# Sparse attention and a PReLU feed-forward on one core: score pieces joined per head pair, crossbar transposes for all four pairs, another order in batches 0 and 1

## The chip, the core and the metric

The kernel runs on one core of one Trainium2 chip. The core has a matrix engine (TensorE, PE in the profile), a vector engine (VectorE, DVE), a scalar engine (ScalarE, ACT), GpSimd (POOL), and a queue processor, SyncE (SP), which here only issues DMAs. The metric is the device time of one execution in microseconds; less is better. Before the change the median of seven runs is 329.11 us (328.95 to 331.41).

## What is computed

Eight batches of eight heads, 576 positions of 64 elements each. The first four heads attend to the last 32 positions (local), the last four to all earlier positions with the same remainder modulo 32 (strided). Softmax, product with v, and then a feed-forward over all 4608 positions with a per-channel leaky slope:

```python
scores = scale * np.matmul(q, k.transpose(0, 1, 3, 2))
mask_local = (rel >= 0) & (rel < stride)                # stride = 32
mask_strided = (rel >= 0) & (pos[None, :] % stride == pos[:, None] % stride)
masks = np.stack([mask_local if h < H // 2 else mask_strided for h in range(H)], axis=0)
scores = np.where(masks[None, :, :, :], scores, -1000000000.0)
attn = exp(scores - max); attn = attn / (sum(attn) + 1e-09)
attn_out = np.matmul(attn, v)
x = attn_out.transpose(0, 2, 1, 3).reshape(B * S, H * D)     # 4608 x 512
h = x @ w_in                                                 # 512 -> 2048
g = np.maximum(h, 0.0) + alpha * np.minimum(h, 0.0)
out = g @ w_out                                              # 2048 -> 512
```

Inputs and output are float32; the kernel works in float16 with float32 sums.

## The kernel before

**Feed-forward.** The 4608 positions are cut into nine chunks of 512. For each chunk `lin1_piece` (L534) makes one of 16 row blocks of h with four 512-column matmuls (the four operands are the four head pairs' rows of xT), ScalarE makes the negative part (L554), and VectorE combines both (L557). `lin2_piece` (L563) makes the output in 16 parts of four matmuls each, a ScalarE copy to osb after every fourth part (L590), and a transfer out on SP's queue (L591). A chunk therefore has 32 slots: 16 of lin1, 16 of lin2. xT is a ring of four batches.

**Attention.** A head pair is two heads side by side on the 128 partitions. Per batch, pairs 0 and 1 are local and pairs 2 and 3 strided; pair number g is 4 x batch + pair. The work on a pair is cut into pieces:

- T (`transpose_piece`, L221): transposes q or k on TensorE into a "ps" buffer, copies by VectorE and ScalarE, and for k the tails. From batch 2 on (DX = 2) the strided q and k come transposed by the DMA crossbar (`load_d` L118 and `transpose_d` L124), so only the local ones have T pieces.
- S (`score_piece`, L275): half of a pair's scores. The operands have 64 rows (one head), so the two heads' matmuls go to the two halves of the array, each to a bank of its own: TensorE is in a row-tiled mode for this. An exponential on ScalarE (L319) follows, and from batch 2 on a mask multiplication on GpSimd (L329). In batches 0 and 1 the mask is added by two more matmuls (L311).
- P (`pv_piece`, L331): product with v, two pieces for a local pair and three for a strided one, into a "ps" buffer; reciprocal and scaling by VectorE (L352, L354) into x16.
- X: the result is transposed into xT, either on TensorE with a copy by ScalarE or VectorE (`x_piece`, L359), or by a crossbar transpose from SP's queue (`x_dma`, L372): straight into xT for local pairs, into xs for strided ones, with a ScalarE copy later (`x_copy`, L381). Before the change pairs 0, 1 and 2 of batches 2 to 7 use the crossbar, pair 3 uses TensorE.

PSUM[...]: three "ps" buffers (T, tails, P, X), three "hps" (lin1, lin2), and one "sp" of two banks (scores).

**Order.** The order is written by hand: `alone` (L406) lists the pieces of batches 0 and 1, and the loop at L449 lists those of later batches. In pass g of that loop, pair g is scored, pair g - 1 gets its products with v, and the next local unit is transposed; `run` (L490) adds to a piece the casts, loads and crossbar transposes that go with it. `attn_step` (L524) issues the next piece after a lin1 or lin2 slot, and then the VectorE part of lin1 that was put off (`late`). Batch 0 runs ahead of all chunks with warm-up matmuls between the pieces (L662); batch 1 in the lin2 half of chunk 0; batch n + 1 in chunk n (L708), paced by

```python
acc += left / (22.5 - 0.5 * skip) * (0.5 if i < 16 else 1.0)
```

so that pieces come half as densely in lin1 as in lin2 and the last one falls about one slot before the end of the chunk. Lin1 of chunk n reads xT of batch n, finished at the end of chunk n - 1. Chunks 7 and 8 have no attention beside them. [...]

Of the kernel before, what the change touches and what calls it, by code (L numbers as in the profile page):

```python
# [31 lines left out]
def kernel(  # L32
# [10 lines left out]
    nc = tc.nc  # L43
# [46 lines left out]
    vls = [cpool.tile([128, 24, 65], F16, name=f"vl{i}") for i in range(2)]  # L90
    vss = [cpool.tile([128, 4, 8, 65], F16, name=f"vs{i}") for i in range(2)]
    ets = [cpool.tile([128, 640], F16, name=f"et{i}") for i in range(NE)]
    x16s = cpool.tile([80, 1024], F16)
    qks = {nm: cpool.tile([80, 4, 512], F16, name=f"{nm}sd") for nm in "qk"}


# [105 lines left out]
    def make_pair(g):  # L202
        P = Pair()
        P.g, P.b, P.hp = g, g // 4, g % 4
        P.strided = P.hp >= 2
        P.pr = P.hp % 2
        P.n, P.w = (8, 72) if P.strided else (6, 96)
        u = g // 2
        P.dx = P.b >= DX and P.strided
        P.xd = P.b >= DX and P.hp < 3  # L210
        if P.dx:
            P.qT, P.kT = (z[u % 2].rearrange("r e c -> r (e c)") for z in (qTs, kTs))
        else:
            P.qT, P.kT = qTs[u % 2][:, g % 2], kTs[u % 2][:, g % 2]
        P.sgroups = ([0, 1, 2, 3], [4, 5, 6, 7]) if P.strided else ([0, 1, 2], [3, 4, 5])
        P.pgroups = ([0, 1, 2], [3, 4, 5], [6, 7]) if P.strided else P.sgroups
        P.et = {}
        P.x16 = None
        return P
# [55 lines left out]
    def score_piece(P, i):  # L275
# [52 lines left out]
            m = (mstr if P.strided else mother).unsqueeze(1).to_broadcast([r, 2 * n // w, w])  # L328
        keep(nc.gpsimd.tensor_tensor(ev, ev, m, op=ALU.mult))  # L329

    def pv_piece(P, a):  # L331
        if P.x16 is None:
            if P.xd and P.strided:
                P.x16 = x16s
            else:
                P.x16 = xpool.tile([128, 1024], F16, tag="x16", name="x16")
        v16 = cast16[(P.b, P.strided, "v")]
        grp = P.pgroups[a]
        r = 72 if P.strided else 128
        pv = pspool.tile([128, 512], F32, tag="ps", name="pv")  # L340
        nb = 2 * len(grp)
        for x in range(nb):
            t, hh = grp[x // 2], x % 2
            et, c = P.et[(t, hh)]
            keep(nc.tensor.matmul(  # L345
                pv[:, 65 * x : 65 * x + 65], et[0:r, c : c + 128],
                v16[0:r, 2 * P.pr + hh, t, :] if P.strided else v16[:, 6 * (2 * P.pr + hh) + t, :],
                start=(x == 0), stop=(x == nb - 1), skip_group_check=True))
        w = P.w
        rc = rpool.tile([128, 8], F32, tag="rc", name="rc")  # L350
        pvv = pv[0:w, 0 : 65 * nb].rearrange("r (c e) -> r c e", e=65)
        keep(nc.vector.reciprocal(rc[0:w, 0:nb], pvv[:, :, 64]))  # L352
        c0 = 128 * grp[0]
        keep(nc.vector.tensor_tensor(  # L354
            P.x16[0:w, c0 : c0 + 64 * nb].rearrange("r (c e) -> r c e", e=64),
            pvv[:, :, 0:64],
            rc[0:w, 0:nb].unsqueeze(2).to_broadcast([w, nb, 64]), op=ALU.mult))

    def x_piece(P):  # L359
        xp = pspool.tile([128, 1024], F16, tag="ps", name="xp")  # L360
        for t in range(P.n):
            keep(nc.tensor.transpose(  # L362
                xp[:, P.w * t : P.w * t + P.w], P.x16[0 : P.w, 128 * t : 128 * t + 128], ident[0 : P.w, 0 : P.w]))
        base = (P.b % 4) * S
        if P.strided:
            keep(nc.scalar.copy(  # L366
                xT[:, P.hp, base : base + S].rearrange("r (p t) -> r p t", t=8),
                xp[:, 0:576].rearrange("r (t p) -> r p t", t=8)))
        else:
            keep(nc.vector.tensor_copy(xT[:, P.hp, base : base + S], xp[:, 0:576]))  # L370

    def x_dma(P):  # L372
        base = (P.b % 4) * S
# [29 lines left out]
    def X(g):  # L403
        return lambda: x_piece(pairs[g])

    def alone(u0, u1, ahead):  # L406

        A, L = (2 * u0, 2 * u0 + 1), (2 * u1, 2 * u1 + 1)
        feed(T(u0, "q"), -1)
        feed(T(u0, "k"), -1)  # L410
        for g in A:
            for i in range(2):
                feed(Sc(g, i), -1)
        if ahead:
            feed(T(u1, "q"), -1)
            feed(T(u1, "k"), -1)
            for i in range(2):
                feed(Sc(L[0], i), -1)
        for g in A:
            for i in range(3):  # L420
                feed(Pv(g, i), -1)
        if not ahead:
            feed(T(u1, "q"), -1)
            feed(X(A[0]), -1)
            feed(T(u1, "k"), -1)
            feed(X(A[1]), -1)
            for i in range(2):
                feed(Sc(L[0], i), -1)
        for i in range(2):
            feed(Sc(L[1], i), -1)  # L430
        if ahead:
            for g in A:
                feed(X(g), -1)
        for g in L:
            for i in range(2):
                if g == L[0] and i == 0:
                    feed(lambda: (over_v(u0 // 2, "dve"), pv_piece(pairs[L[0]], 0)), -1)
                else:
                    feed(Pv(g, i), -1)
        for g in L:  # L440
            feed(X(g), -1)

    alone(1, 0, True)
    end0 = len(pieces)
    alone(3, 2, True)
    end1 = len(pieces)


    for g in range(7, npair + 2):  # L449
        c = g // 4  # L450
        a, p, t = g, g - 1, g + 1
        okA = 8 <= a < npair
        okP = 8 <= p < npair
        okT = 8 <= t < npair and (t % 4 == 0 or t < 4 * DX and t % 2 == 0)
        nP = len(pairs[p].pgroups) if okP else 0
        seq = []
        if okA:
            seq.append(("S", Sc(a, 0)))
        if okP:
            seq.append(("P", Pv(p, 0)))  # L460
        if okT:
            seq.append(("T", T(t // 2, "q")))
        if 8 <= g - 2 < npair and not pairs[g - 2].xd:
            seq.append(("X", X(g - 2)))
        if okA:
            seq.append(("S2", Sc(a, 1)))
        if okP:
            seq.append(("P", Pv(p, 1)))
        if okT:
            seq.append(("Tk", T(t // 2, "k")))  # L470
        if nP == 3:
            seq.append(("P", Pv(p, 2)))
        if not seq:
            seq.append(("N", lambda: None))

        todo = [(c, pr) for pr in range(2)] if g % 4 == 0 and 8 <= g < npair else []

        if g % 4 == 1 and 9 <= g and c + 1 < B:
            todo = [(c + 1, nm) for nm in "qk"]
        lastP = max([i for i, z in enumerate(seq) if z[0] == "P"], default=len(seq) - 1)  # L480
        copyP = next((i for i, z in enumerate(seq) if z[0] == "S2"), 0)
        nslots = [i for i, z in enumerate(seq) if z[0][0] != "S"] or list(range(len(seq)))
        for i, (kind, fn) in enumerate(seq):
            extra = []
            if todo and i in nslots:
                left = len([z for z in nslots if z >= i])
                cnt = -(-len(todo) // max(1, left))
                extra = [todo.pop(0) for _ in range(min(cnt, len(todo)))]

            def run(fn=fn, extra=extra, g=g, c=c, kind=kind, lastp=(i == lastP), copyp=(i == copyP)):  # L490
                fn()
                for b, pr in extra:
                    if pr in ("q", "k"):
                        cast_l(b, pr)
                        if b + 1 < B:
                            load_qk(b + 1, False, pr)
                        continue
                    cast_v(b, pr, "pool")
                    if pr == 1 and b + 1 < B:
                        load_v(b + 1, True)  # L500
                if kind == "Tk" and g % 4 == 3 and c + 3 < B:
                    load_tail(c + 3, False)
                if lastp:
                    if 4 * DX <= g - 1 < npair and pairs[g - 1].xd:
                        x_dma(pairs[g - 1])
                    if g % 4 == 0 and DX <= c < B:
                        transpose_d()
                    if g % 4 == 2 and DX <= c and c + 1 < B:
                        load_d(c + 1)
                    if g % 4 == 2 and c + 2 < B:  # L510
                        load_v(c + 2, False)
                if copyp and 4 * DX <= g - 2 < npair and pairs[g - 2].xd and pairs[g - 2].strided:
                    x_copy(pairs[g - 2])
            feed(run, g - 2 if kind == "X" else -1)

    pos = {"i": 0}

# [6 lines left out]
    def attn_step(end):  # L524
# [2 lines left out]
            pos["i"] += 1  # L527
        while late:
            late.pop(0)()


    gTs = {}
# [86 lines left out]
    keep(nc.vector.memset(wrm, 0.0))  # L619
    for nm in "qk":  # L620
        keep(nc.vector.memset(qks[nm][64:80], 0.0))
    keep(nc.vector.memset(x16s[64:80], 0.0))
    keep(nc.sync.dma_start(consts, consts_dram))
    load_qk(0, True, "q")
    load_qk(0, True, "k")
# [129 lines left out]
```

The softmax here doesn't subtract the row's maximum and nothing guards it: scores larger than these inputs give would overflow.

## Time and profile before

| from the profiled execution | |
|---|---|
| its own time | 329.18 us |
| span | 327.2 us |
| TensorE busy | 317.2 us (97%) |
| VectorE / ScalarE / GpSimd busy | 182.6 / 172.6 / 141.4 us |
| lin2 matmuls (L585) | 560, 137.7 us |
| lin1 matmuls (L544) | 640, 133.5 us |
| score matmuls (L295), 72 and 96 columns wide, in sp | 392, 16.9 us |
| exponentials (L319) | 56, mean 646 ns |
| mask multiplications (L329) | 48, mean 1276 ns |
| ScalarE copy xs to xT (L383) | 6, mean 1301 ns |
| ScalarE copy PSUM to xT (L366) | 10, mean 644 ns |
| crossbar transposes xs<-x16s, issue to landing | 6, median 2.7 us |

A line of the timeline gives start, duration (both us), engine, source line, operation, result and operands, shapes, and the number of instructions merged; in brackets, how long the engine was idle before and what ended that. In the chain of work that ended last, each step is followed back to what released it. Matmuls overlap, so their durations add up to more than the time they take: the distance between starts is the measure.

### The profile page before, as it was taken

The numbers are of one execution on the slowest core, as the hardware profiler recorded it, in microseconds if no ns is written. First come the engines' busy times: TensorE is split into PE (matmuls) and PEld (weight loads), VectorE is DVE, ScalarE is ACT, GpSimd is POOL, SyncE is SP. The second block draws the span as 40 slices with busy tenths as digits, with TensorE's granted clock in tenths as the row PEclk, the third lists the DMA queues.
The fourth block names the chain that finished last, engine by engine and source line by source line (L and its number), as shares of the span: only waits on it lengthen the run. The fifth ranks groups of instructions, "written<-read, shape, count | busy, mean of one in ns | idle before, by whom it ended". The sixth has DMA issues, their size and how long they took to land.

```text
span 327.2 us, 6269 instructions
## 1 busy us (share of the span) xinstructions
PE 317.2 (97%) x2493; PEld 161.8 (49%) x2493; DVE 182.6 (56%) x358; ACT 172.6 (53%) x295; POOL 141.4 (43%) x152
## 2 busy tenths in 40 slices
PE   7899999999997999999999999999999999999995
PEld 2454455554553445444558754445444454444444
DVE  5477835577543882388328833783377338505801
ACT  2744663368346754575467645764567346415610
POOL 8832495307996365736573638342512300000000
PEclk9999999999999999999999999999999999999999
DMA  7999999897598899695968496635440320021011
GB/s 224 198 205 206 242 181 191 122 263 158 103 163 128 220 75 159 93 237 68 164 105 227 54 139 118 115 39 105 119 76 3 52 89 29 1 89 40 2 64 64
DMA packets 77596, 40.32 MB, mean 123 GB/s; under 512 B 58480, under 2 KB 69248, under 8 KB 77568
## 3 DMA queue, kind: packets, MB, share of 16 engines
q0 software_dynamic: 41728, 17.38, 51.6%
q1 hardware_dynamic: 35840, 22.55, 29.2%
q8 instruction: 19, 0.31, 0.4%
q14 instruction: 9, 0.07, 0.1%
HBM read 38.01 MB, written 9.44 MB: 145 GB/s over the span
## 4 chain that ended last, share of the span: by engine, by line
PE 92%; DVE 2%; ACT 2%; DMA 2%; issue 1%; SPq 0%; DVEq 0%; ACTq 0%
PE hps L544 38%; PE ops L585 37%; PE sp L295 4%; PE pv L345 4%; PE tp L235 2%; DMA ql<-in_q_dram 2%; PE wps L607 1%; PE ops L577 1%; PE xp L362 1%; DVE x L354 1%; PE sph L311 1%; PE sp L311 1%; ACT kT L175 1%; DVE qT L177 1%; PE sph L295 1%
## 5 line engine op out<-in xcount | busy, mean ns | idle before, releaser
L585 PE MATMUL ops<-wout,gT 128*128 128x512 f16 x560 | 137.7, 379 | 0.0
L557 DVE SCALAR_TENSOR_TENSOR gT<-neg,oma,hps 128x512 f16<-128x512 f32 x144 | 106.0, 745 | 55.3 <-ACT neg L554 47.7
L544 PE MATMUL hps<-xT,win 128*128 128x512 f16 (+1 forms) x640 | 133.5, 358 | 1.8 <-ACT xT L366 1.2
L554 ACT ACTIVATE neg<-hps 128x512 f32<-128x512 f32 x144 | 86.0, 597 | 41.0 <-PE hps L544 39.4
L329 POOL TENSOR_TENSOR et<-et,consts 128x576 f16<-128x576 f16 (+1 forms) x48 | 61.2, 1276 | 92.3 <-ACT et L319 92.2
L544 PEld LDWEIGHTS <-win 128*128 128x128 f16 x640 | 59.6, 98 | 58.2 <-issue 3.2
L585 PEld LDWEIGHTS <-gT 128*128 128x128 f16 x560 | 48.5, 98 | 45.5
L319 ACT ACTIVATE et<-sp 72x576 f16<-72x576 f32 (+1 forms) x56 | 36.2, 646 | 45.0 <-PE sp L295 36.7
L352 DVE RECIPROCAL rc<-pv 72x6 f32<-72x6 f32 (+2 forms) x80 | 14.8, 185 | 51.2 <-PE pv L345 51.2
L590 ACT COPY osb<-ops 128x512 f32<-128x512 f32 x35 | 20.5, 587 | 31.6 <-PE ops L585 31.2
L354 DVE TENSOR_TENSOR x<-pv,rc 96x384 f16<-96x384 f32 (+2 forms) x62 | 33.0, 532 | 2.1
L345 PEld LDWEIGHTS <-et 72*128 72x128 f16 (+1 forms) x448 | 23.2, 98 | 16.2 <-DVE x L354 1.1
L295 PEld LDWEIGHTS <-kT 64*128 64x128 f16 x448 | 10.8, 95 | 25.8 <-issue 20.7
L295 PE MATMUL sp<-qT,kT 64*128 64x72 f16 (+1 forms) x392 | 16.9, 201 | 1.9 <-ACT kT L175 1.9
L607 PE MATMUL wps<-wrm 128*128 128x512 f16 x44 | 16.3, 444 | 1.2 <-DVE wrm L619 1.2
L345 PE MATMUL pv<-vs,et 72*128 72x65 f16 x256 | 15.3, 194 | 0.1
L167 POOL DMA_DIRECT2D vl<-in_v_dram x8 | 11.2, 1394 | 9.8 <-PE pv L345 8.4
L179 POOL COPY vs<-stv 72x1024 f16<-72x1024 f16 x14 | 14.5, 1038 | 0.0
L177 DVE COPY qT<-tp 128x1024 f16<-128x1024 f16 (+1 forms) x10 | 10.1, 1012 | 7.6 <-PE tp L235 7.6
L383 ACT COPY xT<-xs 128x576 f16<-128x576 f16 x6 | 7.8, 1301 | 8.2 <-DMA xs<-x16s 8.2
L345 PE MATMUL pv<-vl,et 128*128 128x65 f16 x192 | 10.8, 194 | 0.0
L175 ACT COPY kT<-tp 128x1024 f16<-128x1024 f16 (+1 forms) x10 | 8.4, 843 | 3.9 <-PE tp L235 3.9
(72 smaller groups left out, 162.5 us busy)
## 6 DMA issues: line engine op xcount, KB each, us to landing
out_dram<-osb SPq DMA_DIRECT2D x35, 256.0 KB, 2.2
ql<-in_q_dram SPq DMA_DIRECT2D x6, 512.0 KB, 4.9
kl<-in_k_dram SPq DMA_DIRECT2D x6, 512.0 KB, 5.4
stv<-in_v_dram POOLq DMA_DIRECT2D x8, 288.0 KB, 6.4
vl<-in_v_dram POOLq DMA_DIRECT2D x6, 384.0 KB, 10.7
win<-in_moe_w_in_dram POOLq DMA_DIRECT2D x4, 512.0 KB, 9.4
wout<-in_moe_w_out_dram POOLq DMA_DIRECT2D x4, 512.0 KB, 16.5
qsd<-in_q_dram POOLq DMA_DIRECT2D x6, 288.0 KB, 5.7
```

What stands on the lines that cost most here:

```text
L295: keep(nc.tensor.matmul(sps[y][:, w * x : w * x + w], P.kT[hf, k0 : k0 + 128], P.qT[hf, q0 : q0 + w], start=(x == 0), stop=(x == len(grp) ...
L319: keep(nc.scalar.activation(ev.rearrange("r (y c) -> r y c", y=2), sp[0:r, :, 0:n], AF.Exp, scale=SCALE))
L329: keep(nc.gpsimd.tensor_tensor(ev, ev, m, op=ALU.mult))
L345: keep(nc.tensor.matmul(pv[:, 65 * x : 65 * x + 65], et[0:r, c : c + 128], v16[0:r, 2 * P.pr + hh, t, :] if P.strided else v16[:, 6 * (2 * ...
L352: keep(nc.vector.reciprocal(rc[0:w, 0:nb], pvv[:, :, 64]))
L354: keep(nc.vector.tensor_tensor(P.x16[0:w, c0 : c0 + 64 * nb].rearrange("r (c e) -> r c e", e=64), pvv[:, :, 0:64], rc[0:w, 0:nb].unsqueeze ...
L544: keep(nc.tensor.matmul(hps[:, dst : dst + w], win16[:, kk, 128 * m : 128 * m + 128], xT[:, kk, src : src + w], start=(kk == 0 and x == 0) ...
L554: keep(nc.scalar.activation(neg, hps, AF.Relu, scale=-1.0))
L557: keep(nc.vector.scalar_tensor_tensor(gTs[n][:, m, :], neg, oma[:, m : m + 1], hps, op0=ALU.mult, op1=ALU.add))
L585: keep(nc.tensor.matmul(ops, gTs[n][:, kf, 128 * mt : 128 * mt + 128], wout16[:, kf, :], start=(kf == 0), stop=(kf == 15)))
L590: keep(nc.scalar.copy(osb, ops))
L607: keep(nc.tensor.matmul(wps, wrm[:, 0:128], wrm, start=True, stop=True))
```

## The change

- In `alone`, batches 0 and 1: the P pieces of the strided pairs are placed between the T pieces and the scores of the local pairs, `over_v` comes with the first P of the second strided pair, and X pieces between P pieces. The option `ahead` goes.
- From batch 2 on, `score_both` issues both score pieces of a pair in one piece. The first half goes to "sp" as before; the second to two "ps" buffers, with one exponential for each head, put off to the following calls of `attn_step` (or to a P piece that needs them). The mask of the second half follows its second exponential.
- Pair 3 of batches 2 to 7 is also transposed by the crossbar. x16s becomes two buffers. The two copies from xs into xT are issued in the last pass of the batch (g % 4 == 1): pair 2's after its first piece, pair 3's after its last one.
- The local v load of a batch, from batch 4 on, is issued one batch ahead at g % 4 == 1, where it was two ahead at g % 4 == 2.
- In batches 0 and 1, the copy of pair 0's result goes to ScalarE.

```diff
-    x16s = cpool.tile([80, 1024], F16)
+    x16s = [cpool.tile([80, 1024], F16, name=f"x16s{i}") for i in range(2)]
...
-        P.xd = P.b >= DX and P.hp < 3
+        P.xd = P.b >= DX
...
+    defer, defer_et = [], {}
+
+    def score_both(P):
+
+        w, r = P.w, 72 if P.strided else 128
+        for i in range(2):
+            et = ets[ectr["i"] % NE]
+            ectr["i"] += 1
+            if i:
+                sps = [pspool.tile([128, 512], F32, tag="ps", name="sph") for _ in range(2)]
+            else:
+                sp = pbpool.tile([128, 2, 512], F32, tag="sp", name="sp")
+                sps = [sp[:, y] for y in range(2)]
+            grp = P.sgroups[i]
+            n = w * len(grp)
...
+            if i == 0:
+                keep(nc.scalar.activation(
+                    ev.rearrange("r (y c) -> r y c", y=2), sp[0:r, :, 0:n], AF.Exp, scale=SCALE))
+                keep(nc.gpsimd.tensor_tensor(mv, mv, m, op=ALU.mult))
+                continue
+
+            def ex(y):
+                keep(nc.scalar.activation(
+                    ev[:, n * y : n * y + n], sps[y][0:r, 0:n], AF.Exp, scale=SCALE))
+                if y:
+                    keep(nc.gpsimd.tensor_tensor(mv, mv, m, op=ALU.mult))
+
+            defer_et["et"] = et
+            defer.extend([lambda: ex(0), lambda: ex(1)])
+
     def pv_piece(P, a):
+        while defer and any(P.et[z][0] is defer_et["et"] for z in P.et):
+            defer.pop(0)()
...
-                P.x16 = x16s
+                P.x16 = x16s[P.pr]
...
-            keep(nc.vector.tensor_copy(xT[:, P.hp, base : base + S], xp[:, 0:576]))
+            cast_copy("act" if P.b < NEARLY and P.hp == 0 else "dve",
+                      xT[:, P.hp, base : base + S], xp[:, 0:576])
...
-    def alone(u0, u1, ahead):
+    def alone(u0, u1):
...
+        fns = [T(u0, "q"), T(u0, "k")] + [Sc(g, i) for g in A for i in range(2)]
+        fns += [Pv(A[0], 0), T(u1, "q"), Pv(A[0], 1), T(u1, "k"), Pv(A[0], 2), Sc(L[0], 0), Sc(L[0], 1)]
+        fns += [lambda: (over_v(u0 // 2, "dve"), pv_piece(pairs[A[1]], 0)), Sc(L[1], 0), Pv(A[1], 1)]
+        fns += [Sc(L[1], 1), Pv(A[1], 2), Pv(L[0], 0), X(A[0]), Pv(L[0], 1), X(A[1])]
+        fns += [Pv(L[1], 0), Pv(L[1], 1), X(L[0]), X(L[1])]
...
-            seq.append(("S", Sc(a, 0)))
+            seq.append(("S", lambda a=a: score_both(pairs[a])))
...
-        if okA:
-            seq.append(("S2", Sc(a, 1)))
...
-                    if g % 4 == 2 and c + 2 < B:
-                        load_v(c + 2, False)
-                if copyp and 4 * DX <= g - 2 < npair and pairs[g - 2].xd and pairs[g - 2].strided:
+                    if g % 4 == 1 and DX < c and c + 1 < B:
+                        load_v(c + 1, False)
+                if first and g % 4 == 1 and 4 * DX <= g - 3 < npair:
+                    x_copy(pairs[g - 3])
+                if last and g % 4 == 1 and 4 * DX <= g - 2 < npair:
                     x_copy(pairs[g - 2])
-            feed(run, g - 2 if kind == "X" else -1)
+            feed(run, g - 2 if i == len(seq) - 1 else -1)
...
         while late:
             late.pop(0)()
+        if defer:
+            defer.pop(0)()
...
-    keep(nc.vector.memset(x16s[64:80], 0.0))
+    for t in x16s:
+        keep(nc.vector.memset(t[64:80], 0.0))
```

More of the change, by code (lines that the diff above doesn't have):

```diff
@@ L329, in score_piece @@
         keep(nc.gpsimd.tensor_tensor(ev, ev, m, op=ALU.mult))
+    defer, defer_et = [], {}
[11 more added lines that the diff above has]
+            n = w * len(grp)
+            for x, t in enumerate(grp):
+                if P.dx:
+                    q0 = k0 = 80 * (4 * (2 * P.pr + t % 2) + t // 2)
+                else:
+                    q0, k0 = w * t, 32 + 72 * t if P.strided else 96 * t
+                for y in range(2):
+                    hf = slice(64 * y, 64 * y + 64)
+                    keep(nc.tensor.matmul(
+                        sps[y][:, w * x : w * x + w], P.kT[hf, k0 : k0 + 128],
+                        P.qT[hf, q0 : q0 + w], start=(x == 0), stop=(x == len(grp) - 1),
+                        skip_group_check=True))
+                    P.et[(2 * (t // 2) + y, t % 2) if P.strided else (t, y)] = (et, n * y + w * x)
+            ev = et[0:r, 0 : 2 * n]
+            if not P.strided and i == 0:
+                mv = ev.rearrange("r (y c) -> r y c", y=2)
+                m = mfirst.unsqueeze(1).to_broadcast([r, 2, n])
+            else:
+                mv = ev.rearrange("r (c f) -> r c f", f=w)
+                m = (mstr if P.strided else mother).unsqueeze(1).to_broadcast([r, 2 * n // w, w])
+            if i == 0:
[10 more added lines that the diff above has]
+            defer.extend([lambda: ex(0), lambda: ex(1)])
@@ L404, in X @@
         return lambda: x_piece(pairs[g])
-    def alone(u0, u1, ahead):
+    def alone(u0, u1):
         A, L = (2 * u0, 2 * u0 + 1), (2 * u1, 2 * u1 + 1)
[L409 to L443, printed above, removed]
+        fns = [T(u0, "q"), T(u0, "k")] + [Sc(g, i) for g in A for i in range(2)]
[3 more added lines that the diff above has]
+        fns += [Pv(L[1], 0), Pv(L[1], 1), X(L[0]), X(L[1])]
+        for fn in fns:
+            feed(fn, -1)
+    alone(1, 0)
     end0 = len(pieces)
-    alone(3, 2, True)
+    alone(3, 2)
     end1 = len(pieces)
@@ L480 @@
         lastP = max([i for i, z in enumerate(seq) if z[0] == "P"], default=len(seq) - 1)
-        copyP = next((i for i, z in enumerate(seq) if z[0] == "S2"), 0)
         nslots = [i for i, z in enumerate(seq) if z[0][0] != "S"] or list(range(len(seq)))
@@ L488, with run @@
                 extra = [todo.pop(0) for _ in range(min(cnt, len(todo)))]
-            def run(fn=fn, extra=extra, g=g, c=c, kind=kind, lastp=(i == lastP), copyp=(i == copyP)):
+            def run(fn=fn, extra=extra, g=g, c=c, kind=kind, lastp=(i == lastP), first=(i == 0), last=(i == len(seq) - 1)):
                 fn()
```

## The prediction

> **What bounds the kernel now.** I read the page's busy table and its 40 slices first, then the chain that ended last, then TensorE's own order of time in a middle chunk. From the page:
>
> ```profile
> span 327.2 us, 6269 instructions
> PE 317.2 (97%) x2493; PEld 161.8 (49%) x2493; DVE 182.6 (56%) x358; ACT 172.6 (53%) x295; POOL 141.4 (43%) x152
> ...
> PEclk9999999999999999999999999999999999999999
> ...
> PE 92%; DVE 2%; ACT 2%; DMA 2%; issue 1%; SPq 0%; DVEq 0%; ACTq 0%
> ```
>
> TensorE carries 92% of the chain at full clock, and no other engine is busy above 56%. So time falls only where TensorE has less to do or loses a wait. A busy TensorE says little about work, since ends are modelled; I count start to start instead. TensorE in order of time:
>
> ```profile
> 135.29 0.42 PE L362 MATMUL xp<-consts,x 72*128 72x72 f16 x8
> 135.55 1.03 PE L585 MATMUL ops<-wout,gT 128*128 128x512 f16 x4
> 136.42 2.75 PE L544 MATMUL hps<-xT,win 128*128 128x512 f16 x12
> ...
> 153.20 1.03 PE L585 MATMUL ops<-wout,gT 128*128 128x512 f16 x4
> 154.06 0.61 PE L235 MATMUL tp<-consts,ql 128*128 128x128 f16 x8
> 154.51 1.03 PE L585 MATMUL ops<-wout,gT 128*128 128x512 f16 x4
> 155.47 0.30 PE L295 MATMUL sp<-qT,kT 64*128 64x72 f16 x8
> 155.71 1.04 PE L585 MATMUL ops<-wout,gT 128*128 128x512 f16 x4
> ```
>
> Four 512-column matmuls take 0.86 (153.20 to 154.06) ahead of a full-array group, but 0.96 (154.51 to 155.47) ahead of a score piece: entering costs 0.10. The piece then takes 0.24 to the next group's start. A score visit is 0.34 us. A transposed result (xp) takes 0.26, with no loss around it. Chunks without attention take 27.6; a middle one 33.5 (136.42 to 169.93).
>
> Two other stretches have waits. At the end of chunk 1 ScalarE, then TensorE:
>
> ```profile
> 100.79 1.31 ACT L383 COPY xT<-xs 128x576 f16<-128x576 f16 x1 [4.30 <-DMA xs<-x16s]
> 102.00 0.58 ACT L590 COPY osb<-ops 128x512 f32<-128x512 f32 x1
> 102.48 0.66 ACT L319 ACTIVATE et<-sp 128x576 f16<-128x576 f32 x1
> 103.02 0.64 ACT L366 COPY xT<-xp 128x576 f16<-128x576 f16 x1
> ```
> ```profile
> 102.15 0.38 PE L544 MATMUL hps<-xT,win 128*128 128x512 f16 x1 [0.47 <-ACT xT L383]
> 103.71 0.59 PE L544 MATMUL hps<-xT,win 128*128 128x512 f16 x2 [1.19 <-ACT xT L366]
> ```
>
> The copy of a crossbar result stood at the head of ScalarE's queue, and everything behind it was late: from 101.29 on, the chain leaves TensorE and comes back at 103.71, about 2.1 us after the two matmuls at 101.09 were through. In the start of batch 0, scores wait for kT and the last transposes for VectorE:
>
> ```profile
> 16.12 0.30 PE L295 MATMUL sp<-qT,kT 64*128 64x96 f16 x6 [0.90 <-ACT kT L175]
> ...
> 26.28 0.30 PE L362 MATMUL xp<-consts,x 96*128 96x96 f16 x3 [0.39 <-DVE x L354]
> ```
>
> **What the Trainium skill says.** "TensorEngine Tiling (Array Packing)", Key Properties: changing the tiling mode, not just the tile, drains TensorE. The trace agrees: 0.96 against 0.86. "TensorE: Matmul & The Clock Gate", Architectural detail: ScalarE and VectorE run strictly in order. The 4.30 us above shows it. "DMA: Bandwidth & Descriptors", Issuing engines are not separate DMA queues: transfers of all issuers share 16 engines. The crossbar transposes of x16s landed after 2.6 to 3.6 us five times, and after 6.8 once, when the DMA row was full from 90 to 99 us.
>
> **The change, part by part**, against the profiled execution's 329.18 us (span 327.2 and 1.98 around it; the median of the runs, 329.11, is the same within 0.1).
>
> *One visit a pair.* 24 pairs (batches 2 to 7) go from two visits to one. The second piece's eight matmuls cost what the first's do inside the mode: the eight weight loads at 155.46 span 0.18 (six of 96 columns: 0.16). A joint visit is 0.10 + 0.24 + 0.17 = 0.51 in place of 0.68. Saved: 24 x 0.17 = 4.1. Low end: only the entry is saved, 24 x 0.10 = 2.4; high end: exit overhead is larger and inner work smaller, 24 x 0.2 = 4.8. I take 4.1.
>
> The second piece's scores now sit in two of the three "ps" buffers that PV, transposes and tails share. A PV two pieces later needs the first of them, so its exponential must be done. ScalarE after a visit runs the first exponential (0.65), at the last visit of a batch also a copy of xs (1.30), then two halves (0.41 each): the first half is read 2.5 us after the visit, while that PV comes 0.86 + 1.05 + 0.86 = 2.8 after it with an empty slot between. In chunk 1, which has denser pieces, there is no empty slot: 1.9 against 2.5, a stall of 0.6. ScalarE gains 24 x (0.65 + 2 x 0.41 - 2 x 0.65) = 4 us of work over the kernel, under 53% busy. The masks on GpSimd keep number and size; PV reads them a loop later.
>
> *Crossbar for pair 3.* Six xp pieces leave TensorE: 6 x 0.26 = 1.6 saved. Six ScalarE copies from PSUM (0.64) become copies from xs (1.30), and SP issues six more transposes (1.20 each), ahead of the two qT/kT transposes and the next out transfer; those have chunks of slack and three osb buffers. A second x16s memset (0.49 on VectorE) falls into its 1.39 us wait for q at 6.16.
>
> *Copies at the end of the batch.* Pair 2's copy comes later, seven slots after its transpose instead of about four. Without its vl load in the way the chunk-1 wait should shrink. But pair 3's copy is now the last thing before lin1. 21 pieces a batch become 16; with the pacing rule, pair 3's last PV falls in lin2 slot 26 and the copy in slot 30. From that PV's start: VectorE makes x16s and SP issues 0.99 later (159.05 to 160.04 for pair 2), landing 2.7 later: 3.7. ScalarE is free at about 4.4 (out copy, exponential, pair 2's copy, two halves), so the copy ends at 5.7. Lin1 of the next chunk reads pair 3 as its fourth operand at 0.12 + 1.38 + 0.86 + 1.05 + 1.05 + 0.86 + 0.65 = 5.97. It fits by 0.2. I book 0.4 lost over chunks 2 to 5. Chunk 1 has one slot less: about 0.9 lost including the 0.6 above, against 2.1 now: 1.2 saved. In chunk 6 (no new scores, 11 pieces) the last PV is in slot 28 and the copies in slot 30: landing 3.7, copy to 5.0, needed at 0.12 + 3 x 0.86 + 0.65 = 3.4: 1.6 lost. Chunks 7 and 8 are untouched.
>
> *load_v of the local half* moves from one loop to three loops later and one batch closer. Its GpSimd issue (1.46) now stands behind the q/k casts at the batch's end; the next mask is two slots away. Data are wanted a whole chunk later and land in 10.3. Cost nothing; if its 10 us of traffic met pair 3's transpose it would cost as the rival below, but it is issued after that one should land.
>
> *Order in batches 0 and 1.* The 26 pieces and their warm matmuls stay; strided PVs fill VectorE between the local transposes. Walking batch 0 through with the durations of the page (PV 0.19, VectorE 0.74 a PV, kT/qT copies 0.59 to 0.69, tails waiting for a ps buffer until about 16.1): first local scores at 17.0 instead of 16.12, but no block of six strided PVs after them, and the last copy at 25.8 instead of 27.07. Saved 1.2; bounds 0 and 3.2 (13.7 us from 13.4 to 27.13 against 10.5 of TensorE work). Batch 1 loses its 0.47 wait for kT at 51.55: 0.4 saved.
>
> *Sum:* 4.1 + 1.6 + 1.2 + 1.2 + 0.4 = 8.5 saved, 1.6 + 0.4 = 2.0 lost: 329.2 - 6.5 = **322.7 us**.
>
> **Rivals.** *Late crossbar at each boundary (slower).* My budget is a landing within 5.97 - 1.30 - 0.06 - 0.99 = 3.6 us of the issue. For: kT/qT transposes take 6.2 to 6.6 at the median and the local xT ones 5.1, with a strided v load issued about when pair 3's goes. Against: that load's data start after most of pair 3's 2.7 us, and the long ones followed heavier loads. At 5.1, five boundaries lose 1.5 and the last 4.0: 8.5 gained, 11.5 lost, 332.2. It decides for slower from about 5 us. *Small drains.* A joint visit saves only the entry (2.4), the start nothing: 3.3 less gain, 326.0. For: row-paired matmuls may not pipeline further than eight. Against: 0.18 for eight loads. *The visit waits.* TensorE waits inside the visit for a ps buffer that a PV or a transpose still holds: 0.2 at each of 24 eats 4.8: 327.5 to 328.5, no measurable change. Against: VectorE frees a PV after 0.74, a slot is 0.86 or more.
>
> **How the numbers follow.** Forecast's case 0.72 (own range 320 to 325), small drains 0.14, waiting visit 0.05, late crossbar 0.09. A difference of 0.5% (1.65 us) is about what a measurement of this kernel can tell from none. Faster: 0.72 + 0.14 = 0.86; same 0.05; slower 0.09. The range, 319.5 to 327.0, takes the start's and the visit's bounds (start 3.2, visit 4.8: about 2.7 lower, with some of the 2.0 losses staying) and the small-drain case; it leaves out the late crossbar and half of the waiting visit.
>
> **What would show it.** Right: 24 TensorE groups of L295 shape with 12 or 16 matmuls, about 0.41 from start to next group; middle chunks of about 32.6 instead of 33.5 (four visits 0.68, one xp 0.26, less 0.1); lin1 of chunk 0 starting near 25.9; a wait of lin1 for the copy from xs of about 1.6 near 261 us and of little elsewhere. Wrong: such a wait of over 1 us at most boundaries, landings of xs above 4 us, or idle TensorE inside the score groups with a PV's or exponential's release behind it.

## The result, and the profile after

The changed kernel takes 337.58 us (median of 12 runs, 334.0 to 342.5) against 329.22 before (31 runs). The ratio is 1.0207, with a 95% interval of 1.0177 to 1.0237: slower by about 2%, where 2% faster was forecast. The runs spread more than those of before, with mean granted clocks from 0.975 to 0.995, and the ratio leaves out those over 1.5% above the fastest, which is why it is below the quotient of the medians.

The page of the changed kernel, profiled at 337.59 us:

```profile
span 335.8 us, 6240 instructions
PE 314.3 (94%) x2445; PEld 161.5 (48%) x2445; DVE 183.7 (55%) x357; ACT 176.6 (53%) x321; POOL 140.7 (42%) x152
...
PEclk9999999999999999879999999999999999999999
...
PE 75%; DMA 13%; issue 5%; DVE 2%; ACT 2%; POOL 2%; SPq 0%; POOLq 0%; DVEq 0%; ACTq 0%
```

TensorE has less busy time than before (314.3 against 317.2), yet the span is 8.6 us longer. Its share of the chain fell from 92% to 75%, DMA rose from 2% to 13%, and in two slices the clock is below 0.9. The chain names the transfers: xs<-x16s with 6.5% and kT<-ksd with 4.3%. TensorE's waits (us in total, times, longest) say the same:

```profile
PE hps L571 <- ACT xT L435: 11.2, 5, 3.9
PE sp L353 <- DMA kT<-ksd: 2.8, 2, 1.8
```

L571 is the lin1 matmul, L435 the ScalarE copy from xs into xT, L353 a score matmul. The first scores of pair 2, in chunk 3 before and in chunk 2 after:

```profile
143.08 0.30 PE L295 MATMUL sp<-qT,kT 64*128 64x72 f16 x8
106.66 0.30 PE L353 MATMUL sp<-qT,kT 64*128 64x72 f16 x8 [1.81 <-DMA kT<-ksd]
```

Before, a local half came first (at 139.10), and these scores 6.7 us after the chunk's start; now, in chunks 2 to 5, they stand right behind its first twelve matmuls, and the transposes qT and kT must have landed by then. The start of lin1 in each chunk shows where the time goes (us from the span's start, both from TensorE's order of time):

| chunk | before | after | after minus before |
|---|---|---|---|
| 1 | 65.19 | 63.74 | -1.5 |
| 2 | 101.09 | 99.45 | -1.6 |
| 3 | 136.42 | 136.41 | 0.0 |
| 4 | 169.77 | 175.36 | +5.6 |
| 5 | 203.28 | 210.11 | +6.8 |
| 6 | 236.63 | 245.15 | +8.5 |
| 7 | 268.18 | 275.48 | +7.3 |
| 8 | 295.8 | 304.7 | +8.9 |

The losses come right after the boundaries. Chunk 3 is the worst; TensorE there, in order of time:

```profile
135.55 1.03 PE L612 MATMUL ops<-wout,gT 128*128 128x512 f16 x4
136.41 0.81 PE L571 MATMUL hps<-xT,win 128*128 128x512 f16 x3
141.16 4.00 PE L571 MATMUL hps<-xT,win 128*128 128x512 f16 x9 [3.94 <-ACT xT L435]
145.09 0.42 PE L353 MATMUL sp<-qT,kT 64*128 64x72 f16 x8
145.31 0.44 PE L353 MATMUL sph<-qT,kT 64*128 64x72 f16 x8
```

Three matmuls run at once: they read pairs 0, 1 and 2. The fourth reads pair 3 and waits until 141.16. Then nine matmuls take 3.93 us to the next group, 0.44 each, twice the usual 0.216. The same stretch in windows (busy us of each engine, then granted clock, DMA share, GB/s):

```profile
core 0: us, PE busy (x) PEld busy (x) DVE busy (x) ACT busy (x) POOL busy (x), PEclk, DMA share, GB/s
...
139.00:141.00 2.00, 0.00 (x0) 0.00 (x0) 0.00 (x0) 1.19 (x1) 1.10 (x1) 0.62 1.07 100
...
143.00:145.00 2.00, 2.00 (x6) 0.44 (x3) 0.91 (x2) 0.60 (x1) 0.00 (x0) 0.50 1.94 229
```

The clock was halved while TensorE waited, and stayed so for the first matmuls after it. From 0.62 over 139 to 141 it fell at about 139.5, 2.3 us into the idle time; the same view reads 0.67 over 145 to 147, so it was back at about 146.3. "TensorE: Matmul & The Clock Gate" of the Trainium skill says in Part 1 that the clock is halved after an idle window of about 3.4 us. The trace agrees in that idle time of 3.94 us did it here, while 2.49 at chunk 2 did not; but the fall came before 3.4 us of idle time were over.

Why is pair 3 late? SP's queue, GpSimd's and ScalarE's at this boundary, with the line of that transfer (last number: us from issue to landing), and the same for the last boundary that has scores behind it (240.85):

```profile
132.12 1.21 SPq L428 DMA_TRANSPOSE xs<-x16s  x1
132.50 0.81 POOL L159 DMA_DIRECT2D stv<-in_v_dram  x1
xs<-x16s SPq DMA_TRANSPOSE x1, 7.7
139.81 1.30 ACT L435 COPY xT<-xs 128x576 f16<-128x576 f16 x1 [4.54 <-DMA xs<-x16s]
...
240.85 1.21 SPq L428 DMA_TRANSPOSE xs<-x16s  x1
xs<-x16s SPq DMA_TRANSPOSE x1, 2.6
```

At 132 a strided v load is issued 0.4 us after the transpose, which lands after 7.7 us. At 240.85 there is no further batch to load, and it lands after 2.6, although the qT and kT transposes follow there as closely as anywhere.

The saving itself is there. A joint visit, from the same order of time:

```profile
164.06 1.89 PE L612 MATMUL ops<-wout,gT 128*128 128x512 f16 x8
165.88 0.30 PE L353 MATMUL sp<-qT,kT 64*128 64x96 f16 x6
166.02 0.29 PE L353 MATMUL sph<-qT,kT 64*128 64x96 f16 x6
166.25 1.04 PE L612 MATMUL ops<-wout,gT 128*128 128x512 f16 x4
```

Eight matmuls take 1.82 instead of 1.73, so 0.09 to enter; the visit lasts 0.37; together 0.46 against 2 x 0.34.

So the theory to test: a v load beside pair 3's crossbar transpose makes that one late, lin1 waits for it at the boundary, and a long wait halves the clock. Rivals: the three transposes in a row slow each other; the joint visits or the new start cost time themselves.

### The profile page after: what moved, and what is told of

Read it like the earlier page. It is cut to its first block, busy times and chain, and to the rows that moved or that the text cites. A ratio compares the mean times of both kernels' runs of the same rounds, so it can differ in the third digit from the quotient of the medians.

```text
span 335.8 us, 6240 instructions
## 1 busy us (share of the span) xinstructions
PE 314.3 (94%) x2445; PEld 161.5 (48%) x2445; DVE 183.7 (55%) x357; ACT 176.6 (53%) x321; POOL 140.7 (42%) x152
## 4 chain that ended last, share of the span: by engine, by line
PE 75%; DMA 13%; issue 5%; DVE 2%; ACT 2%; POOL 2%; SPq 0%; POOLq 0%; DVEq 0%; ACTq 0%
PE hps L571 32%; PE ops L612 29%; DMA xs<-x16s 7%; DMA kT<-ksd 4%; PE pv L396 4%; DMA kl<-in_k_dram 2%; PE tp L235 2%; PE wps L634 1%; PE sp L353 1%; ACT xT L435 1%; PE ops L604 1%; PE sph L311 1%; PE sp L311 1%; PE sph L353 1%; DVE x L405 1%
## 5 line engine op out<-in xcount | busy, mean ns | idle before, releaser
L571 PE MATMUL hps<-xT,win 128*128 128x512 f16 (+1 forms) x640 | 134.7, 362 | 11.6 <-ACT xT L435 11.2
L584 DVE SCALAR_TENSOR_TENSOR gT<-neg,oma,hps 128x512 f16<-128x512 f32 x144 | 106.3, 745 | 63.4 <-ACT neg L581 54.1
L612 PE MATMUL ops<-wout,gT 128*128 128x512 f16 x560 | 135.2, 379 | 0.0
L571 PEld LDWEIGHTS <-win 128*128 128x128 f16 x640 | 60.7, 98 | 72.3 <-issue 17.0
L612 PEld LDWEIGHTS <-gT 128*128 128x128 f16 x560 | 49.5, 98 | 48.1
L405 DVE TENSOR_TENSOR x<-pv,rc 96x384 f16<-96x384 f32 (+2 forms) x44 | 23.8, 541 | 1.5
L435 ACT COPY xT<-xs 128x576 f16<-128x576 f16 x12 | 15.7, 1308 | 14.5 <-DMA xs<-x16s 14.5
L366 ACT ACTIVATE et<-sp 128x576 f16<-128x576 f32 (+1 forms) x24 | 15.5, 646 | 12.8 <-PE sp L353 12.8
L405 DVE TENSOR_TENSOR x16s<-pv,rc 72x384 f16<-72x384 f32 (+1 forms) x36 | 18.3, 509 | 1.2
L372 ACT ACTIVATE et<-sph 128x288 f16<-128x288 f32 (+1 forms) x48 | 18.6, 408 | 0.0
L353 PEld LDWEIGHTS <-kT 64*128 64x128 f16 x336 | 7.3, 97 | 13.2 <-issue 8.5
```

What stands on the lines that cost most here:

```text
L372: keep(nc.scalar.activation(ev[:, n * y : n * y + n], sps[y][0:r, 0:n], AF.Exp, scale=SCALE))
L405: keep(nc.vector.tensor_tensor(P.x16[0:w, c0 : c0 + 64 * nb].rearrange("r (c e) -> r c e", e=64), pvv[:, :, 0:64], rc[0:w, 0:nb].unsqueeze ...
L435: keep(nc.scalar.copy(xT[:, P.hp, base : base + S].rearrange("r (p t) -> r p t", t=8), P.xs[:, :, 0:72].rearrange("r t p -> r p t")))
L571: keep(nc.tensor.matmul(hps[:, dst : dst + w], win16[:, kk, 128 * m : 128 * m + 128], xT[:, kk, src : src + w], start=(kk == 0 and x == 0) ...
L584: keep(nc.vector.scalar_tensor_tensor(gTs[n][:, m, :], neg, oma[:, m : m + 1], hps, op0=ALU.mult, op1=ALU.add))
L612: keep(nc.tensor.matmul(ops, gTs[n][:, kf, 128 * mt : 128 * mt + 128], wout16[:, kf, :], start=(kf == 0), stop=(kf == 15)))
```

## The experiments

**Take the v load away from the transpose.** One edit of the changed kernel (run e1_v_load_apart):

```diff
                     cast_v(b, pr, "pool")
-                    if pr == 1 and b + 1 < B:
-                        load_v(b + 1, True)
...
                     if g % 4 == 2 and DX <= c and c + 1 < B:
                         load_d(c + 1)
+                        load_v(c + 1, True)
```

> The changed kernel with one edit: the strided v load of the next batch is issued at g % 4 == 2, beside the qsd/ksd loads, instead of next to pair 3's crossbar transpose. Theory (the v load slows that transpose): xs lands after 2.6 to 3 us at every boundary, lin1 waits for the copy from xs under 0.5 us except 1.5 before chunk 7, no wait for kT, clock 1.00; of some 17 us of waits about 3 stay: 324 us. Rival (the two qT/kT transposes behind it slow it): landings stay above 5 us and the time within 2 us of 337.6.

325.75 us, ratio to before 0.9886 (0.9852 to 0.9921), clock 0.999: 1.75 above the number of the theory. Almost 12 us went with one load's place. TensorE's waits, and the one of 2.4 us in order of time:

```profile
PE hps L570 <- ACT xT L435: 2.8, 3, 1.5
PE pv L396 <- ACT et L372: 2.4, 1, 2.4
...
PE sp L353 <- DMA kT<-ksd: 0.7, 1, 0.7
...
99.70 0.34 PE L396 MATMUL pv<-vl,et 128*128 128x65 f16 x6 [2.37 <-ACT et L372]
```

That wait (0.3 in the changed kernel) belongs to batch 2: the moved load goes out 2.8 us ahead of pair 2's transpose there, which lands after 7.7 us instead of 5.7; its copy holds up the put-off exponentials behind it on ScalarE.

**Move the neighbouring transposes instead** (run e6_qk_transposes_early): the v load stays, the qT/kT transposes go four slots ahead.

```diff
-                    if g % 4 == 0 and DX <= c < B:
-                        transpose_d()
...
+                if first and g % 4 == 0 and DX <= c < B:
+                    transpose_d()
```

> The changed kernel with one edit: the qT/kT transposes are issued at the first piece of pass g % 4 == 0, four slots ahead of pair 3's crossbar transpose instead of right behind it; the v load stays. Theory (the v load slows xs): landings of pair 3 stay at 5 to 8 us, only the waits for kT (2.8 us) go: 334 to 336 us. Rival (the neighbouring transposes slow xs): landings 2.6 to 3 us, 324 to 326 us.

337.15 us, ratio 1.0269 (1.0195 to 1.0342), about 1 us above the theory's range. The waits for kT are gone, but lin1 waits 12.1 us for the copies, once 5.4, and the clock is 0.99 in the profiled execution. The 5.4 are before chunk 2: the two moved transposes stand ahead of pair 3's on SP's queue there, so that it goes out at 98.86 instead of 95.79. Landings of pair 3's transpose by batch (us from issue):

| kernel | batch 2 | 3 | 4 | 5 | 6 | 7 |
|---|---|---|---|---|---|---|
| changed kernel (v load 0.4 after it in 3 to 5, 1.0 in 2; none in 6, 7) | 5.6 | 7.7 | 5.9 | 5.1 | 2.6 | 2.6 |
| qT/kT transposes early (v load the same in 3 to 5) | 5.7 | 5.0 | 6.5 | 5.1 | 2.7 | 2.6 |
| v load apart | 5.6 | 4.5 | 2.7 | 2.7 | 2.6 | 2.6 |

The rival of the neighbouring transposes falls: in batches 3 to 5 the landing stays late without them, and in batches 4 and 5 it is 2.7 without the load. Batch 2 does not tell, since other loads are in flight in all three (with the v load apart it lands at 96.3, and two small ones at 98.1 and 98.3, around a transpose issued at 95.04). The 4.5 in batch 3 has no GpSimd transfer beside it; what slowed it is open.

**Put the v load beside a transpose in the kernel before** (run e3_before_v_load_close):

```diff
-                    if pr == 1 and b + 1 < B:
-                        load_v(b + 1, True)
...
                 if lastp:
+                    if g % 4 == 3 and DX <= c and c + 1 < B:
+                        load_v(c + 1, True)
                     if 4 * DX <= g - 1 < npair and pairs[g - 1].xd:
                         x_dma(pairs[g - 1])
```

> The kernel before with one edit: the strided v load is issued at the same piece as pair 2's crossbar transpose (and no longer a pass later). Theory (v load slows a neighbouring transpose): xs lands after 5 to 8 us instead of 2.7 in batches 2 to 6, still 2.7 in batch 7; the copy on ScalarE waits 1 to 4 us a batch; 330 to 334 us. Rival: landings stay at 2.6 to 3.6, the time at 329.

333.49 us, ratio 1.0102 (1.0072 to 1.0133). Pair 2's transpose lands after 7.9, 5.6, 5.4, 5.1, 3.7 and 2.6 us, against 6.8, 3.6, 2.6, 2.7, 2.7 and 2.7 before. The load went out 0.9 us ahead of it in batches 3 and 4, and 2.2 ahead in 5 and 6, where the 3.7 of batch 6 is less than expected. The effect on the landing is shown in a kernel without any other part of the change. The profiled execution was the quickest of the eleven, with a span of 328.4, so where the slower ones lose their time is not shown.

**Pair 3 back on TensorE** (run e2_pair3_on_tensor):

```diff
-        P.xd = P.b >= DX
+        P.xd = P.b >= DX and P.hp < 3
...
-                if last and g % 4 == 1 and 4 * DX <= g - 2 < npair:
+                if last and g % 4 == 1 and 4 * DX <= g - 2 < npair and pairs[g - 2].xd:
                     x_copy(pairs[g - 2])
```

> The changed kernel with pair 3 of batches 2 to 7 transposed on TensorE and copied from PSUM, as before the change; all else stays. Theory (the loss is the wait for pair 3 at the boundaries): about 14 us of waits and slow clock go and 1.6 us of transposes come back: 325 us, perhaps 2 us more where kT is still late. Rival (the joint score visits or the new order of the start cost time themselves): 330 us or more.

324.54 us, ratio 0.9852 (0.9824 to 0.988), clock 1.00. All but pair 3's crossbar makes the kernel faster. The kT transposes still meet the v load here (7.2 to 8.1 us in batches 3 to 5), and TensorE waits only 0.4 for them.

**Does the wait halve the clock?** (run e9_fill) Matmuls whose result nobody reads fill part of the wait:

```diff
         while pos["i"] < ab:
             attn_step(ab)
+        if 1 <= n <= 4:
+            fill = phpool.tile([128, 512], F32, tag="hps", name="fill")
+            for _ in range(8):
+                keep(nc.tensor.matmul(fill, wrm[:, 0:128], wrm, start=True, stop=True))
```

> The changed kernel with eight more 512-column matmuls (1.7 us, result unused) at the end of chunks 1 to 4, where TensorE waits 1.5 to 4 us for pair 3. Theory (a wait of about 4 us halves the granted clock for some us): the work fits into the waits, the clock stays at 1.00, 333 to 336 us, and the times of the runs lie closer together than 334 to 342. Rival (the clock falls for another reason): clock 0.98 to 0.99 as before, 338 to 341 us.

334.14 us (333.62 to 336.04), ratio 1.0155 (1.0109 to 1.0201), clock 1.00. TensorE at the boundary that was worst before:

```profile
134.49 1.89 PE L756 MATMUL fill<-wrm 128*128 128x512 f16 x8
136.21 2.78 PE L571 MATMUL hps<-xT,win 128*128 128x512 f16 x12
140.05 0.30 PE L353 MATMUL sp<-qT,kT 64*128 64x72 f16 x8 [1.06 <-DMA kT<-ksd]
```

More matmuls, and yet 3.4 us less than the median of the changed kernel, with a narrow spread. Here the transpose also landed after 5.0 instead of 7.7 us, so this one boundary is no clean pair; the clock (0.995 to 1.00 in the four runs, 0.975 to 0.995 in the twelve of the changed kernel) and the spread over all runs are the evidence. Between the two profiled executions lin1's waits fell from 11.2 to 2.9 us. The filling takes 6.9 of these 8.3, so 1.4 us is shorter waiting, and the clock's part, by the nine matmuls above, is 2.0: 3.4 of the 4.0 us by which the spans differ.

**The joint visits alone, on the kernel before** (run e4_before_joint_scores):

```diff
-            seq.append(("S", Sc(a, 0)))
+            seq.append(("S", lambda a=a: score_both(pairs[a])))
...
-        if okA:
-            seq.append(("S2", Sc(a, 1)))
...
-        copyP = next((i for i, z in enumerate(seq) if z[0] == "S2"), 0)
+        copyP = next((i for i, z in enumerate(seq) if z[0] == "P"), 0)
...
+        if defer:
+            defer.pop(0)()
```

With the second score piece gone, pair 2's copy from xs needs another place: it comes with the first P piece of the same pass, earlier than before.

> The kernel before with only the joint score visits (two ps buffers, exponentials put off) from batch 2 on; pair 3 stays on TensorE, the start and the loads stay. A visit of two halves took 0.10 + 0.37 us in the changed kernel, against 2 x 0.34: theory 24 x 0.21 = 5.0 us less, 324 us. Rival (waits for ps buffers inside or after the visits take it back): 327 to 329 us with TensorE waiting for PV's or exponentials' releases.

331.33 us, ratio 1.0055 (1.0036 to 1.0073): the expectation failed. One event in batch 2 stands out; ScalarE and then TensorE, in order of time:

```profile
101.14 1.30 ACT L434 COPY xT<-xs 128x576 f16<-128x576 f16 x1 [7.08 <-DMA xs<-x16s]
102.35 0.41 ACT L372 ACTIVATE et<-sph 128x288 f16<-128x288 f32 x1
```
```profile
97.12 0.30 PE L353 MATMUL sp<-qT,kT 64*128 64x96 f16 x6
102.80 0.42 PE L353 MATMUL sph<-qT,kT 64*128 64x96 f16 x6 [5.39 <-ACT et L372]
103.16 1.89 PE L636 MATMUL ops<-wout,gT 128*128 128x512 f16 x4
```

Pair 2's transpose landed after 8.6 us, behind the qsd, ksd and local v loads. Its copy stood at the head of ScalarE, a put-off exponential behind it, and that held the "ps" buffer which the next visit's second half needs. TensorE stood for 5.39 us within the visit, and the four matmuls after it take 1.68 (103.16 to 104.84) instead of 0.86: the clock again. So the third rival of the prediction, the waiting visit, exists, but once in this kernel, and behind an exponential with a DMA at its root. The earlier place of the copy is part of this edit: ScalarE began to wait 1.6 us after the transpose was issued, against 2.6 in the kernel before, and in the change the copy comes a pass later. What that place adds to the wait was not tested.

**The same with that local v load moved as in the change** (run e11_joint_scores_v_load_later):

```diff
-                    if g % 4 == 2 and c + 2 < B:
-                        load_v(c + 2, False)
+                    if g % 4 == 1 and DX < c and c + 1 < B:
+                        load_v(c + 1, False)
```

> The kernel before with the joint score visits and the later local v load of the change, nothing else. With the joint visits alone, one wait of 5.4 us in batch 2 and the clock after it hid the gain: pair 2's transpose landed after 8.6 us behind that v load, its copy stood at the head of ScalarE, and the put-off exponentials held the ps buffers. Theory: that landing falls to about 5 us, the wait to under 2 us, clock 1.00: 326 us. Rival (the joint visits themselves wait): 329 us or more.

327.65 us, ratio 0.9933 (0.9909 to 0.9958). The landing fell to 5.6, the wait to 2.3. The median is 1.65 us above the theory's number and 1.35 below the rival's, so neither came out as written; but it is faster than before beyond doubt. With the landing time 3.0 us shorter and the copy in the same place, the wait is 3.1 shorter and the time 3.7 less.

**The new start alone** (run e5_before_new_start): only the order of `alone` and pair 0's copy there, as in the diff of the change.

> The kernel before with only the new order of batches 0 and 1 and pair 0's copy there on ScalarE. In the changed kernel lin1 of chunk 0 starts at 25.8 us and that of chunk 1 at 63.7 instead of 27.1 and 65.2: theory 1.4 us less, 327.7 us. Rival: within 0.3 us of before, since the later chunks wait for loads anyway.

327.49 us, ratio 0.995 (0.9932 to 0.9968): 1.65 us saved. (The first lin1 matmul starts at 26.64 before and 25.35 in the changed kernel; the expectation's 27.1 and 25.8 are the ends of batch 0's last copies, 27.07 and 25.79. The difference is the same.)

**Both cures at once** (run e8_v_apart_pair3_on_tensor): the edits of the v load apart and of pair 3 on TensorE together.

> The changed kernel with pair 3 back on TensorE and the strided v load moved to g % 4 == 2. If both the neighbour of the transposes and the missing slack at the boundary are out of the way: kT not waited for, 0.3 to 1.5 us less than with pair 3 on TensorE alone: 323.5 us, clock 1.00. Rival (the v load now meets the local pairs' transposes): 325 us or more.

328.22 us, ratio 0.996 (0.994 to 0.9979), worse than either. The rival's time came, but not by what it named: the second local pair's transposes of batches 3 to 6 do land later (7.0 to 9.0 us against 5.2 to 6.7), yet no wait of TensorE has one behind it. In batch 2 the moved load now goes out 3.7 us ahead of pair 2's transpose, which lands after 7.6 us (4.9 without the move); TensorE waits 3.5 us in one place behind put-off exponentials, and the clock is 0.99. ScalarE and TensorE there:

```profile
98.80 1.30 ACT L435 COPY xT<-xs 128x576 f16<-128x576 f16 x1 [3.08 <-DMA xs<-x16s]
100.46 0.64 PE L413 MATMUL xp<-consts,x 72*128 72x72 f16 x8 [3.54 <-ACT et L372]
```

This is read from one trace; the next run leaves batch 2's load where it was.

**A version without either collision** (run e10_v_apart_from_batch3): pair 3 on TensorE in batches 2 and 7 only, the v load moved from batch 3 on.

```diff
-        P.xd = P.b >= DX
+        P.xd = P.b >= DX and (P.hp < 3 or P.b not in (DX, B - 1))
...
-                    if pr == 1 and b + 1 < B:
+                    if pr == 1 and b == DX:
                         load_v(b + 1, True)
...
                         load_d(c + 1)
+                        if c > DX:
+                            load_v(c + 1, True)
```

`x_copy` is left out for pairs that go over TensorE, as in the run with pair 3 on TensorE.

> The changed kernel with pair 3 on TensorE in batches 2 and 7 only (on the crossbar in 3 to 6), and the strided v load moved to g % 4 == 2 from batch 3 on. It puts together what the runs point to: no v load beside pair 3's transpose, no wait of the last batch, no load added to the crowded batch 2. Theory: waits of 3 to 4 us in all, clock 1.00, 322.5 to 324 us, below the 324.5 of pair 3 on TensorE throughout. Rival (batch 2's crowd decides and the crossbar for pair 3 gives nothing): 324.5 us or more.

323.01 us (322.93 to 323.27), ratio 0.98 (0.9777 to 0.9824), clock 1.00: faster than both kernels and than every other run. Pair 3's transpose lands after 2.7 us in all four batches that have it, and after 90 us no wait of TensorE is above 0.9. So about what was forecast for the change (322.7) was there to be had, with loads and transposes placed otherwise.

## Why the prediction was wrong

The step that failed is *Copies at the end of the batch*, in its term "landing 2.7 later", with the argument that the v load's data "start after most of pair 3's 2.7 us". The times of issue were nearly right: x16s was ready and the transpose issued 0.99 after the last PV's start, and the v load came 0.4 us later. But the landing was 5.1 to 7.7 us wherever that load was beside it (in batch 2, 5.6 also with the load moved), and with the load moved 2.7 in batches 4 and 5. The prediction had the median of transposes that had no such neighbour, and it treated a load issued behind the transpose as harmless. Its slower rival, *Late crossbar*, named the place, the load and the deciding landing of about 5 us; it got 9%.

- **The boundaries.** 0.4 us were booked for the ends of chunks 2 to 5 together and 0.9 for chunk 1's end. Measured as gaps between groups: 2.6 before lin1 of chunk 2, 4.1 of chunk 3, 2.1 of chunk 4, 1.5 of chunk 5, none in chunk 6. The boundary before chunk 6, with all its scores and no v load, fits: pair 3's copy ends at 245.20 and the fourth matmul starts at 245.79, 0.6 to spare where 0.2 was worked out.
- **What was not in the sum.** The qT/kT transposes were said to have "chunks of slack". The next chunk's first score piece is pair 2's, because the pieces of a batch became fewer, and it reads them: 2.8 us of waits (none in e6, which moves them). And the halved clock: nine matmuls at chunk 3 took 3.93 instead of 1.94, 2.0 us in the profiled execution.
- **Chunk 6's end.** 1.6 lost was forecast before lin1 of chunk 7; the wait is 1.46 in idle time, 1.6 as a gap between groups.
- **Joint visits.** The mechanism was right. A visit's price is 0.46 against 0.51 forecast. Over a middle chunk (203.2 to 236.7 before, 199.8 to 232.7 with pair 3 on TensorE), the time at the score groups and that lost by the matmuls ahead of them fell from 1.86 + 0.78 to 1.45 + 0.67: 0.52 a chunk, 3.1 in six, against 4.1. The rest is in lin1: the twelve matmuls ahead of its second visit take 2.97 us, 0.38 above the pure rate where 0.10 is the price of entry. 0.28 of it is one wait: the ninth of the twelve starts 0.50 after the eighth instead of 0.22, released by VectorE's gT (L584), which had the scaling of a PV before it. A run with another order there was not made. (The middle chunk that the prediction reads as 33.5 is 33.35 long: the next lin1 starts at 169.77, not 169.93.)
- **Pair 3's transposes.** 0.26 a chunk before, gone after: as forecast.
- **The start.** 1.6 forecast, 1.65 measured by e5; the last copy of batch 0 ends at 25.79 in the changed kernel, where 25.8 was forecast.
- **The local v load.** It was booked at nothing. It is worth something in batch 2: without it near pair 2's transpose the kernel with the joint visits alone goes from 331.33 to 327.65 us.

Together: the parts that work on TensorE saved about 1.65 + 3.1 + 1.6, and the waits put on top about 2.6 + 4.1 + 2.1 + 1.5 + 1.6 + 3.0 for kT + 2.0 of clock = 16.9, of which 2.1 at chunk 2 stood there before. 16.9 - 2.1 - 6.4 is 8.4; the spans differ by 8.6.

## What to carry to other kernels

A transfer's landing time belongs to its neighbours: before a DMA is put on the path of the bound engine, list what every queue issues within some microseconds of the new place, and take the duration from a row with the same company, not the median. Where a result goes to the bound engine by way of a DMA and a copy, a margin of 0.2 us is none; move the bulk load, or keep the last piece on the bound engine, as pair 3 here. A copy that waits for a DMA should not stand ahead of work that frees buffers.

## What was not expected of the hardware

- A 288 KB load issued by GpSimd 0.4 us after a crossbar transpose of 80 x 1024 made that land after 4.8 to 7.7 us (batches 3 to 5 of three kernels), where it took 2.6 or 2.7 with the load elsewhere, but for one 4.5. "DMA: Bandwidth & Descriptors" of the Trainium skill says in "Issuing engines are not separate DMA queues" that DMAs of the scalar, sync and GpSimd engines run on the same 16 DMA engines and interleave; a slowdown by 1.8 to 2.9 times, by a load that comes second, was more than I read into it. How the engines share the two is not shown.
- Long gaps of TensorE cost twice. In the four profiles with idle time of 3.5 us or more in one piece (3.94 in the changed kernel, 5.39 in e6 and in e4, 3.54 in e8) the clock fell to 0.50 from 2.2 to 3.8 us into the gap and stayed there for 6.8 us; idle time of up to 2.67 us (e6) left it at 1.00. Matmuls took 0.44 instead of 0.216. With the gap partly filled by eight unread matmuls the kernel was 3.4 us faster at the median.
- The same move of one load, to the same place, saved 12 us in one kernel and cost 3.7 in another (324.54 to 328.22): in the first it freed pair 3's transposes and delayed pair 2's in batch 2 (7.7 us); in the second, with pair 3 on TensorE, only the delay was left (7.6 us).
